# Pairs of token groups in 64x64 quarters instead of single groups, in a retention and MLP kernel

## The chip, the cores and the metric

The kernel runs on one core of one Trainium2 chip. The metric is the device time of one execution in microseconds (us). The four runs of the kernel before lie between 297.73 and 299.04 us. The engines are named as the profile names them: PE is the matrix engine, PEld its weight loads, DVE the vector engine (VectorE in the text), ACT the scalar engine (ScalarE), POOL is GpSimd, SP the engine whose queue (SPq) issues most of the DMA transfers (186 of the 196 issues counted in the trace of the kernel before). "Clock" is the PE clock that the profile gives as granted: 1.0 is full speed.

## The reference

The reference is a decayed, causal attention without a softmax, and an MLP with the activation h cos(h). There are 8 sequences of 576 tokens with 8 heads of 64, so 4608 tokens of 512 features. Cut to what matters:

```python
scores = scale * np.matmul(q, k.transpose(0, 1, 3, 2))
gamma = 1.0 - 2.0 ** (-5.0 - np.arange(H, dtype=np.float32))
Dmat = np.where(rel >= 0, gamma[:, None, None] ** rel[None, :, :], 0.0)
ret = scores * Dmat[None, :, :, :]
attn_out = np.matmul(ret, v)                  # 8 x 8 x 576 x 64
x = attn_out.transpose(0, 2, 1, 3).reshape(B * S, H * D)
h = x @ w_in                                  # 4608 x 2048
g = h * np.cos(h)
out = g @ w_out                               # 4608 x 512
```

## The kernel before

The decay is split into a factor for the query and one for the key, so that only a triangular mask is left for the scores. The tokens are treated in chunks. For a chunk the kernel needs the scores of its own tokens (`sc`), their product with the values (`ov`, "own"), a contribution of all earlier tokens from a state (`ov`, "carried"), and the update of that state (`st`). For all of these the queries and keys are scaled (`qks`) and transposed (`qkT`), in the first groups by PE and later by DMA transfers; this is what "transposes" means below. The result `xT` feeds the first product of the MLP (`h`), ScalarE and VectorE make `gT` of it, and the second product (`o`) follows. PE writes its products into banks of the PSUM memory (named by letters), and here a bank is written again only after its content has been read. The tokens run through the MLP in ten passes of 512, 256, 256 and seven times 512 tokens. From pass 3 on, the second product uses seven half-size products instead of eight; the sums that this needs (`gs`) are made on VectorE and GpSimd.

Before the change a chunk is a group of 128 tokens, one token per partition.

```python
    def load(g, names="qkv", gate=None):          # cut
        for name in names:
            f = ld.tile([P, H, D], F32, tag="f" + name, name=f"f{name}")
            for p0, p1, t in parts:
                b, s0 = divmod(t, S)
                i = nc.sync.dma_start(
                    f[p0:p1], src[b, :, s0 : s0 + p1 - p0, :].rearrange("h s d -> s h d")
                )

    def prep(g, early=False, kv_first=False):     # cut: scales q and k into bf16, copies v
        if not early and not kv_first:
            scaled(nc.gpsimd, 0, tiles.pop(("fq", g)), gq)
        scaled(nc.vector if g == 3 else nc.gpsimd, 1, fk, gk)
        ...

    def scores(g, bank, idle=0, parts=1, put_off=None):   # cut
        warm(ps[:, 0].rearrange("p b i -> p (b i)"), idle)     # dummy matmuls on zeros
        for hg in range(HG):
            for i0 in range(0, P, P // parts):
                for he in range(2):
                    d0, i1 = he * D, i0 + P // parts
                    nc.tensor.matmul(
                        ps[i0:i1, he, hg, :],
                        lhsT=qkT[d0 : d0 + D, HG + hg, i0:i1],
                        rhs=qT[d0 : d0 + D, hg, :],
                        start=True, stop=True)

    def mm1(n, et, c0, w, bank, inside={}):       # first product of the MLP
        m = 1024 // w
        ps = psum.tile([P, m, w], F32, tag=bank, name="h")
        for j in range(m):
            if j in inside:
                inside[j]()
            for dg in range(DG):
                nc.tensor.matmul(ps[:, j, :],
                    lhsT=w_in_sb[:, dg, (et + j) * P : (et + j + 1) * P],
                    rhs=xT[:, dg, c0 : c0 + w],
                    start=(dg == 0), stop=(dg == DG - 1))
        nc.scalar.activation(cosh, ps, ACTF.Sin, bias=half_pi, scale=1.0)
        nc.vector.tensor_mul(gT[:, et : et + m, c0 : c0 + w], ps, cosh)

    # the start: groups 0 to 3 one by one, with dummies that keep PE busy
    warm(psum.tile([P, 512], F32, tag="n", name="idle"), 14)
    ...
    prep(0, early=True)
    transposes(0, "nn", only=(1,))
    scores(0, "a", idle=2)
    for g in range(G4):
        ...
        w_dma += [load_w_in(e, e + 512) for e in ((0,), (512,), (1024, 1536), ())[g]]
        if g == 2:
            w_dma += [load_w_out(e, e + 4) for e in range(0, ET, 4)]
            load(4, gate=w_dma[5])            # not before the weights
            load(5)
        if g + 1 < G4:
            state(g)
            transposes(g + 1, "nn", only=(1,))
            if g + 2 < G4:
                prep(g + 2, early=True)
            scores(g + 1, "ab"[(g + 1) % 2], idle=3)
            attn_out([g], "m", evac=nc.scalar.copy)
    for g in (4, 5):
        prep(g)                               # on GpSimd
    # the passes follow: mm1 of pass 0 and so on
```

## Time and profile before

| | before |
|---|---|
| time, median of 3 runs | 297.98 us (297.73 to 299.04) |
| span of the profiled run | 296.6 us, clock 1.000 |
| PE busy | 285.2 us, 96% |
| VectorE, ScalarE, GpSimd busy | 70%, 46%, 67% |
| first `h` matmul | 17.61 us |

The first lines are from the page of the kernel before. Its first line gives the busy time of each engine, the share of the span, and the number of instructions. Below are slices: each digit is one fortieth of the span, in tenths of busy time (9 is 90% or more), for PE, for the granted PE clock, and for the DMA engines.

```profile
PE 285.2 (96%) x3091; PEld 195.6 (66%) x3113; DVE 208.9 (70%) x245; ACT 135.9 (46%) x167; POOL 199.7 (67%) x163
...
PE   7899999999989999999999999999999999999995
...
PEclk9999999999999999999999999999999999999999
DMA  8999999999999999999999999997850260021013
```

PE is nearly always busy and always at full clock. The DMA engines are busy nearly to the full through the 27th slice, some 200 us, and then the loads are over. The view of waits, for PE alone, gives what PE stood for, in total, how often, and the longest:

```profile
PE idle L185 <- DVE zeros L660: 1.3, 1, 1.3
PE sc L195 <- DMA qkT<-qks: 1.2, 1, 1.2
PE o L515 <- DVE ot L557: 1.0, 4, 0.4
...
```

So PE waits for about 6 us in all, and the longest wait is 1.3 us. A change helps if it shortens the PE stream or the start. The timeline of PE gives start, duration, the line, what is written and read, the PE tile (rows times columns), the shape, the count, and in brackets the idle time before it with its cause. First pass 0:

```profile
17.61 1.05 PE L365 MATMUL h<-xT,w_in_sb 128*128 128x256 bf16 x8
...
19.49 13.26 PE L365 MATMUL h<-xT,w_in_sb 128*128 128x256 bf16 x120
32.59 9.88 PE L382 MATMUL o<-w_out_sb,gT 128*128 128x512 bf16 x44
```

The first product of pass 0 starts at 17.61 us and the second at 32.59 us. The stretch of retention of one late pair of groups, between two products of pass 7, is:

```profile
223.48 0.44 PE L266 MATMUL st<-vb,qks 128*64 128x64 bf16 x16
223.75 0.62 PE L333 MATMUL ov<-ret,vb 128*64 128x128 bf16 x16
224.30 0.42 PE L319 MATMUL ov<-qkT,sb 64*64 64x128 bf16 x16
224.54 0.62 PE L195 MATMUL sc<-qkT 64*64 64x128 bf16 x32
225.09 0.94 PE L515 MATMUL o<-w_out_sb,gT 128*128 128x256 bf16 x7
```

It lasts from 223.48 to 225.09 us, 1.61 us. Four groups of matmuls stand in it, two in 128x64 tiles and two in 64x64 quarters. This is the time that the change wants to shorten.

### The profile page before, as it was taken

Reading aid. Unit: us, or ns where it says so; the run is one execution under the profiler, and the core shown is the slowest. Engines: PE = TensorE matmul, PEld = TensorE weight load, DVE = VectorE, ACT = ScalarE, POOL = GpSimd, SP = SyncE. Lnnn points to the kernel's source line nnn. Section 1 sums busy time; section 2 is a strip of 40 time slices with the busy share of each in tenths; the row PEclk is TensorE's granted clock in tenths of the full one; section 3 lists DMA queues with packets and bytes.
Section 4 is the critical chain, followed back from the end, with each engine's and each line's share of the span. In section 5 each row is a group of like instructions: output and inputs, shape, how many; then the busy total and the mean of one; then the engine's idle time right before and its main releaser. Section 6 shows DMA issues by size and latency. Waiting matters only on the chain. (4 is left out here: it accounts for less than half of the span.)

```text
span 296.6 us, 7311 instructions
## 1 busy us (share of the span) xinstructions
PE 285.2 (96%) x3091; PEld 195.6 (66%) x3113; DVE 208.9 (70%) x245; ACT 135.9 (46%) x167; POOL 199.7 (67%) x163
## 2 busy tenths in 40 slices
PE   7899999999989999999999999999999999999995
PEld 3478646848568887468745784488448844884594
DVE  6677647564669995688758975897589758935873
ACT  3656432605236532663256355636464446425620
POOL 2750056544445789999999998599859935970583
PEclk9999999999999999999999999999999999999999
DMA  8999999999999999999999999997850260021013
GB/s 208 213 210 207 210 197 201 210 210 232 201 160 232 199 243 231 216 283 160 198 217 254 212 213 221 200 223 194 180 140 2 73 144 0 2 81 62 0 38 106
DMA packets 154304, 50.28 MB, mean 170 GB/s; under 512 B 140832, under 2 KB 153248, under 8 KB 154272
## 3 DMA queue, kind: packets, MB, share of 16 engines
q1 hardware_dynamic: 149504, 45.10, 77.9%
q0 software_dynamic: 4224, 4.19, 8.5%
q8 instruction: 24, 0.39, 0.5%
q10 hardware_dynamic: 544, 0.52, 0.5%
q14 instruction: 8, 0.07, 0.1%
HBM read 36.70 MB, written 9.44 MB: 156 GB/s over the span
## 5 line engine op out<-in xcount | busy, mean ns | idle before, releaser
L443 POOL TENSOR_TENSOR gs<-gT 128x1024 bf16<-128x1024 bf16 x51 | 107.1, 2131 | 36.1 <-DVE gs L443 35.5
L365 PE MATMUL h<-xT,w_in_sb 128*128 128x512 bf16 (+2 forms) x820 | 126.8, 313 | 1.3 <-DVE xT L350 0.7
L374 DVE TENSOR_TENSOR gT<-h,cosh 128x1024 bf16<-128x1024 f32 x72 | 87.9, 1223 | 45.5 <-ACT cosh L373 43.0
L373 ACT ACTIVATE cosh<-h,half_pi 128x1024 f32<-128x1024 f32 x72 | 80.2, 1114 | 66.9 <-PE h L365 66.9
L365 PEld LDWEIGHTS <-w_in_sb 128*128 128x128 bf16 x832 | 75.9, 98 | 49.5 <-issue 1.0
L140 POOL TENSOR_TENSOR qks<-fq,gq 128x512 bf16<-128x512 f32 x32 | 34.2, 1068 | 40.0 <-DMA fq<-in_q_dram 33.7
L515 PEld LDWEIGHTS <-gs 128*128 128x128 bf16 x576 | 53.9, 98 | 9.5 <-issue 1.7
L140 POOL TENSOR_TENSOR qks<-fk,gk 128x512 bf16<-128x512 f32 x35 | 37.7, 1076 | 9.4 <-DMA fk<-in_k_dram 8.8
L207 DVE TENSOR_TENSOR ret<-sc,tri 128x1024 bf16<-128x1024 f32 x32 | 38.1, 1215 | 2.7 <-PE sc L195 2.7
L515 PE MATMUL o<-ws,gs 128*128 128x256 bf16 (+1 forms) x352 | 38.8, 268 | 0.1
L382 PE MATMUL o<-w_out_sb,gT 128*128 128x512 bf16 x120 | 28.9, 380 | 0.5 <-issue 0.2
L515 PE MATMUL o<-w_out_sb,gs 128*128 128x256 bf16 x224 | 26.3, 272 | 1.0 <-DVE ot L557 1.0
L515 PE MATMUL o<-w_out_sb,gT 128*128 128x256 bf16 x224 | 26.3, 273 | 0.0
L535 DVE TENSOR_TENSOR ot<-o,ot 128x512 f32<-128x512 f32 (+2 forms) x25 | 14.9, 603 | 13.9 <-PE o L515 13.8
L515 PEld LDWEIGHTS <-gT 128*128 128x128 bf16 x224 | 21.5, 98 | 4.2
L350 ACT CAST xT<-ov 128x1024 bf16<-128x1024 f32 (+1 forms) x18 | 16.5, 917 | 16.0 <-PE ov L319 13.9
L443 DVE TENSOR_TENSOR gs<-gT 128x1024 bf16<-128x1024 bf16 (+1 forms) x18 | 21.1, 1187 | 0.3
L382 PEld LDWEIGHTS <-gT 128*128 128x128 bf16 x128 | 11.8, 98 | 12.5
L156 POOL CAST vb<-fv 128x512 bf16<-128x512 f32 x22 | 13.8, 628 | 5.1 <-DMA fv<-in_v_dram 3.3
L562 ACT COPY ot<-o 128x512 f32<-128x512 f32 x7 | 4.1, 586 | 20.2 <-PE o L515 20.2
L392 ACT COPY ot<-o 128x512 f32<-128x512 f32 x8 | 4.7, 588 | 18.5 <-PE o L382 18.4
L195 PEld LDWEIGHTS <-qkT 64*64 64x64 bf16 (+1 forms) x512 | 9.0, 105 | 6.1 <-ACT qkT L177 2.3
(70 smaller groups left out, 176.1 us busy)
## 6 DMA issues: line engine op xcount, KB each, us to landing
out_dram<-ot SPq DMA_DIRECT2D x35, 256.0 KB, 4.0
fk<-in_k_dram SPq DMA_DIRECT2D x32, 256.0 KB, 5.1
fv<-in_v_dram SPq DMA_DIRECT2D x32, 256.0 KB, 5.1
fq<-in_q_dram SPq DMA_DIRECT2D x30, 256.0 KB, 4.5
w_in_sb<-in_moe_w_in_dram POOLq DMA_DIRECT2D x4, 512.0 KB, 8.9
w_out_sb<-in_moe_w_out_dram POOLq DMA_DIRECT2D x4, 512.0 KB, 16.3
fq<-in_q_dram SPq DMA_DIRECT2D x8, 128.0 KB, 4.0
fk<-in_k_dram SPq DMA_DIRECT2D x8, 128.0 KB, 4.1
```

The lines of the kernel that those rows point to most:

```text
L140: eng.tensor_tensor(out=qks[:, m].rearrange("p (b a) d -> p a b d", a=2), in0=f.rearrange("p (a b) d -> p a b d", a=2), in1=by[:, c, :].re ...
L156: copy_v(vb, fv)
L195: nc.tensor.matmul(ps[i0:i1, he, hg, :], lhsT=qkT[d0 : d0 + D, HG + hg, i0:i1], rhs=qT[d0 : d0 + D, hg, :], start=True, stop=True,)
L207: nc.vector.tensor_tensor(out=ret.rearrange("p a b i -> p (a b) i"), in0=ps.rearrange("p a b i -> p (a b) i"), in1=mask.unsqueeze(1).to_br ...
L350: evac(tiles["x", n][:, :, t0 : t0 + len(gs) * P], ps.rearrange("p c x i -> p c (x i)"))
L365: nc.tensor.matmul(ps[:, j, :], lhsT=w_in_sb[:, dg, (et + j) * P : (et + j + 1) * P], rhs=xT[:, dg, c0 : c0 + w], start=(dg == 0), stop=(d ...
L373: nc.scalar.activation(cosh, ps, ACTF.Sin, bias=half_pi, scale=1.0)
L374: nc.vector.tensor_mul(gT[:, et : et + m, c0 : c0 + w], ps, cosh)
L382: nc.tensor.matmul(ps, lhsT=gT[:, et, tsi * P : (tsi + 1) * P], rhs=w_out_sb[:, et, :], start=(et == 0), stop=(et == ET - 1),)
L443: i = (nc.vector if on_dve else nc.gpsimd).tensor_tensor(out=tiles["gs", n, x][:, e0:e1], in0=i0, in1=i1, op=op_)
L515: nc.tensor.matmul(dst[i], lhsT=lhs[:, e, j * P : (j + 1) * P], rhs=rhs[:, e, c0:c1], start=(x in (3, 4, 1, 7) and e == 0 and (i == 0 or l ...
L535: pend.append(lambda: nc.vector.tensor_tensor(out=out_, in0=in0, in1=in1, op=op_))
```

## The change

Groups are taken in pairs, 18 of them. In the first six (`FINE = 6`), partition p holds two neighbouring tokens, so one DMA packet has 512 bytes instead of 256 (the page counts 140832 packets under 512 bytes before); their chunks stay at 128 tokens. In the other twelve the chunks shrink to 64 tokens. So less is computed above the diagonal, more states are made, and every product of the retention is a 64x64 quarter of the array, so four of them run beside each other. Some of the half sums move from GpSimd to VectorE, where one takes 0.69 us at the median instead of 2.13 us on average. The start treats pairs 0 and 1 as wholes and has fewer dummies. The diff is long; its core, with cuts marked:

```diff
+    NP = NG // 2
+    QP = P // 4
+    NC = S // HP
+    FINE = 6
-    LD = 5
+    LD = 3
...
-            f = ld.tile([P, H, D], F32, tag="f" + name, name=f"f{name}")
-            for p0, p1, t in parts:
-                b, s0 = divmod(t, S)
+            f = ld.tile([P, H, 2, D], F32, tag="f" + name, name=f"f{name}")
+            for rows, ys, b, s0, cnt in parts:
+                n = ys.stop - ys.start
                 i = nc.sync.dma_start(
-                    f[p0:p1], src[b, :, s0 : s0 + p1 - p0, :].rearrange("h s d -> s h d")
+                    f[rows, :, ys, :].rearrange("p h r d -> p h (r d)"),
+                    src[b, :, s0 : s0 + cnt, :].rearrange("h (p r) d -> p h (r d)", r=n),
                 )
...
+    def prep(G, y, engines=None, copy_v=None):
+        eng = engines or nc.gpsimd
+        if G >= 2:
+            scaled(eng, 0, tiles["fq", G], gq)
+        scaled(eng, 1, tiles["fk", G], gk)
...
+                for hg in range(HG):
+                    for x in range(2):
+                        for he in range(2):
+                            nc.tensor.matmul(
+                                ps[half(x), he, blocks_of(G, u, hg), :],
+                                lhsT=qkT[half(he), u, HG + hg, half(x)],
+                                rhs=queries(G, he, hg, x, yq),
+                                start=True,
+                                stop=True,
+                            )
...
+            for x in range(2):
+                evac(xT[:, x], outs[x])
...
         on_dve = x == 5 or (n, x) == (S7, 2) or (n, x, e0) in (
-            (S7, 1, 4), (last, 1, 0), (last, 2, 4)
-        )
+            (S7, 1, 4), (S7 + 1, 2, 4), (last, 1, 0), (last, 2, 4)
+        ) or (x == 6 and e0 == 0 and S7 < n < last)
...
+    prep(0, 0, copy_v=False)
+    w_dma.append(load_w_in(0, 512))
+    key_transposes(0, "m")
+    masks0 = scores(0, idle=1)
...
+    w_dma += [load_w_in(e, e + 512) for e in (1024, 1536)]
+    w_dma += [load_w_out(e, e + 4) for e in range(0, ET, 4)]
+    load(2, gate=w_dma[5])
+    load(3)
+    load(4)
+    key_transposes(1, "m")
+    run, done = retention(0)
+    run("cross", True)
+    run("own")
+    run("same")
+    done()
+    masks1 = scores(1)
...
+    prep(2, 0)
+    prep(2, 1, nc.vector)
+    prepared = transposed = 6
+    run1, done1 = retention(1, ("n", "st"))
...
             inside = {
-                (0, 0): {2: lambda: (attn_out([3], "n"), state(3))},
-                (1, 0): {4: lambda: scores(5, "a")},
-                (1, 1): {3: lambda: attn_out([5], "a", evac=nc.scalar.copy)},
+                (0, 0): {2: lambda: run1("own"), 3: lambda: run1("same", True)},
+                (0, 1): {0: lambda: (run1("cross"), done1())},
+                (3, 0): {3: lambda: carry(5, ("n", "st"))},
             }.get((n, i), {})
```

## The prediction

It was made from the code, the diff and the profile before, without building the change.

> **What bounds it now.** TensorE. The page's busy table gives PE 285.2 of 296.6 us (96%), at full granted clock in all slices. The waits view, for PE alone, lists only about 6 us of idle: 1.3 before the first matmul, 1.2 on a DMA transpose, 1.0 (four times) on a VectorE add before a product, 0.7 on an xT copy, 0.5 on a state add. The chain of waits is matmuls too. So a saving counts only if it shortens the PE stream, one of these holes, or the start (first h matmul at 17.6 us in the timeline). VectorE is at 70%, GpSimd 67%; the DMA is about 99% busy until some 195 us (slices), yet costs PE only that 1.2 us.
>
> **PE stream of a pair.** In the timeline one late pair (states, values, carried, scores, between two products) lasts 1.5 to 1.7 us, e.g. 223.48 to 225.09. Starts of single matmuls in the trace at 171.3-172.9 us: two 128x64 matmuls of 64 columns every 31 ns, of 128 columns every 56 ns; four 64x64 quarters of 128 columns every 56 ns, of 64 columns every 28 ns. Going from 128x64 to 64x64, and from 64x64 to 128x128, cost about 92 ns more each. [...]
>
> Late pairs (12 of 18), before: states 0.27, values 0.50, carried 0.24, scores 0.50, plus switches: 1.6 us. After: 32 quarters of 64 columns in each of four parts, eight fours at 28-31 ns = 0.24 us each, 0.96, plus two switches: estimate 1.15 us. More instructions, fewer streamed columns. Saving 0.45 x 12 = 5.4 us, all critical.
>
> First six pairs: quarters keep 128 columns: about 1.5 us, as now. Pairs 0-2 now run by single groups in half-array forms (about 2.2 us per pair without transposes): 0.5 us each saved. The 256-token pass in 128-column blocks (128 at 61 ns) becomes 64 at about 110 ns: 0.7 us.
>
> **Others.** The 32 recorded masks of 1.22 us fall to 24; two more state adds per late pair; about six half sums of 2.1 us leave GpSimd for VectorE [...]. Should remove half of the mid-kernel holes (3.7 us): 1.5 us. New holes (a semaphore step between row groups, begin/end splits that switch mode again, sums just in time): minus 1.5 us.
>
> **Start.** Packets go from 256 to 512 bytes: medians in the trace are 18 and 27 ns, so the first keys and values should all land near 13 us, not 16. But a pair now needs both halves' keys scaled, transposed, copied and masked before its first use; first h matmul near 16.5 us, then stalls for pair 1. I credit 0.5 us.
>
> Sum: 5.4 + 1.5 + 0.7 + 1.5 - 1.5 + 0.5 = about 8 us.
>
> **Prediction: 290.0 us, 8 in 10 between 286.0 and 294.5.** Faster by over 2% (below 292.0): 0.72; within 2%: 0.25; slower: 0.03.
>
> **What would show it.** Late retention stretches near 1.15 us; four 64-column quarters every 28-31 ns; first h matmul at 16-17 us; DMA busy share below 90% before 60 us; PE waits 5 us or less in total; 24 masks; N=512 and N=256 matmuls unchanged.
>
> **What would make it wrong.** Quarters of 64 columns with a weight load each may be limited by loads (0.4 us per part would leave no saving). The order of parts may make PE wait for masks or state copies, most in the start and passes 0 to 2. Sums gated behind VectorE could come late for the products. The start could be better than I credit by 2 us.

The sum stays at 8.1 us. Its 0.5 us for each of pairs 0 to 2, its 1.5 us for the mid-kernel holes, its minus 1.5 us for new ones and its 0.5 us for the start were guesses and not read from a trace.

## The result and the profile after

A ratio in this document is the mean time of one kernel's runs over that of the other's runs of the same rounds, so it is not quite the ratio of the medians that stand beside it. Executions over 1.5% slower than the fastest of the same kernel are left out of the means.

| | before | after |
|---|---|---|
| time, median | 298.42 us (297.73 to 299.04, 4 runs) | 322.10 us (321.32 to 323.28, 4 runs) |
| ratio, 95% interval | | 1.0798 (1.0753 to 1.0842) |
| span and clock of the profiled run | 296.6 us, 1.000 | 320.1 us, 0.957 |
| PE busy | 285.2 us | 287.3 us |

The change made the kernel 8% slower, where 290 us were predicted. The same lines of the page after:

```profile
PE 287.3 (90%) x3827; PEld 195.9 (61%) x3848; DVE 199.3 (62%) x252; ACT 148.4 (46%) x194; POOL 190.1 (59%) x173
...
PE   8597059997999989899898998999999999999995
...
PEclk9857659999999999999999999999999999999999
DMA  8999999199999990599959999998793133022003
```

A slice is now 8.0 us. PE has a hole in the fifth and sixth slices, 32 to 48 us. The clock is not full in the second to sixth slices. The waits of PE after:

```profile
PE h L491 <- DVE gT L500: 13.8, 4, 11.5
PE h L491 <- ACT xT L440: 4.1, 3, 1.9
...
```

One wait of 11.5 us is new, on VectorE's `gT`. The timeline of PE in pass 0 of the kernel after shows where:

```profile
18.62 1.87 PE L491 MATMUL h<-xT,w_in_sb 128*128 128x256 bf16 x8
...
26.64 5.21 PE L491 MATMUL h<-xT,w_in_sb 128*128 128x256 bf16 x31 [1.91 <-ACT xT L440]
43.38 11.24 PE L491 MATMUL h<-xT,w_in_sb 128*128 128x256 bf16 x80 [11.53 <-DVE gT L500]
54.45 0.38 PE L508 MATMUL o<-w_out_sb,gT 128*128 128x512 bf16 x1
```

The second product starts at 54.45 us instead of 32.59 us. The wait names VectorE, so the next question is what VectorE waited for. Its timeline in this stretch:

```profile
39.07 0.69 DVE L158 TENSOR_TENSOR qks<-fq,gq 128x512 bf16<-128x512 f32 x1 [18.25 <-DMA fq<-in_q_dram]
41.50 0.69 DVE L158 TENSOR_TENSOR qks<-fk,gk 128x512 bf16<-128x512 f32 x1 [1.74 <-DMA fk<-in_k_dram]
```

VectorE stood for 18.25 us, and not for any `h` that it was to make into `gT`. It stood for the queries of pair 2. Its queue holds `prep(2, 1, nc.vector)` before the first `gT`, because that line is above the loop of passes in the program. The keys of the same pair were issued, in the timeline of the SP queue, at

```profile
32.17 1.53 SPq L137 DMA_DIRECT2D fk<-in_k_dram  x2
```

which is behind the weights, as the gate on `load(2)` wants. The chain of waits, read in order of time (start, length, what), runs through all of it:

```profile
17.69 13.58 DMA w_out_sb<-in_moe_w_out_dram
...
32.17 0.53 SPq L137
32.75 8.66 DMA fk<-in_k_dram
41.50 0.69 DVE qks L158
42.19 1.14 DVE gT L500
43.38 9.50 PE h L491 x64
```

(The short pieces named "issue", and the issue of the load of the queries at 31.29 us, are left out.) Weights, then the issue of the load of pair 2's keys, then their transfer, then the scaling on VectorE, then the first `gT`, then PE. PE could fill three banks with `h` (48 matmuls), and then stood until one was read.

The late stretch of retention of the kernel after, for pass 7 as before:

```profile
248.35 0.32 PE L414 MATMUL ov<-qkT,sb 64*64 64x64 bf16 x16
248.50 0.43 PE L245 MATMUL sc<-qkT 64*64 64x64 bf16 x32
248.80 0.44 PE L414 MATMUL ov<-ret,vb 64*64 64x64 bf16 x32
249.07 0.30 PE L414 MATMUL ov<-qkT,sb 64*64 64x64 bf16 x16
249.20 0.44 PE L316 MATMUL st<-vb,qks 64*64 64x64 bf16 x24
249.56 1.92 PE L643 MATMUL o<-w_out_sb,gT 128*128 128x256 bf16 x16
```

It lasts from 248.35 to 249.56 us, 1.21 us against 1.61 us; the other stretch of this pass takes 1.17 us (254.91 to 256.08) against 1.56 us (230.76 to 232.32). Fours of quarters start every 31 to 33 ns, by the starts of single matmuls in the trace. So the intended gain exists. The starts of the first `h` matmul of each pass, read from the timeline of PE, say where the sum was lost. The two right columns belong to experiments below, E1 and E14.

| start, us | before | after | after minus before | E1 minus before | E14 minus before |
|---|---|---|---|---|---|
| pass 0, `h` | 17.61 | 18.62 | +1.0 | +1.1 | 0.0 |
| pass 0, `o` | 32.59 | 54.45 | +21.9 | +6.3 | 0.0 |
| pass 1, `h` | 48.97 | 73.33 | +24.4 | +8.8 | 0.0 |
| pass 2, `h` | 67.28 | 90.64 | +23.4 | +7.8 | 0.0 |
| pass 3, `h` | 85.06 | 106.96 | +21.9 | +7.5 | -0.7 |
| pass 4, `h` | 116.92 | 140.54 | +23.6 | +9.2 | -0.5 |
| pass 5, `h` | 147.90 | 173.07 | +25.2 | +10.8 | -0.7 |
| pass 6, `h` | 178.14 | 203.94 | +25.8 | +11.6 | +2.7 |
| pass 7, `h` | 207.82 | 232.70 | +24.9 | +10.7 | +1.7 |
| pass 8, `h` | 237.57 | 261.33 | +23.8 | +9.6 | +0.6 |
| end | 296.6 | 320.1 | +23.5 | +9.3 | +0.5 |

Nearly all of the 23.5 us arises before the second product of pass 0. From pass 6 to pass 8 the kernel after wins back 2.0 us for four pairs (59.43 us become 57.39 us), or 0.51 us a pair, near the predicted 0.45 us. By the windows view, 0.40 us of this is a shorter PE stream (58.77 us of busy time in passes 6 and 7 become 57.18 us) and 0.11 us less waiting. But in passes 3 to 5, where six late pairs were to gain as well, it loses 3.9 us more. The windows view for these three passes (start and end, length, then busy time of PE, PEld, DVE, ACT, POOL with counts, the clock, the DMA share, GB/s; this share adds up the times of all packets that start in the window, so it can pass 1), first before, then after:

```profile
85.06:116.92 31.86, 31.58 (x449) 27.02 (x448) 25.86 (x34) 15.42 (x19) 23.69 (x19) 1.00 1.23 216
116.92:147.90 30.98, 30.36 (x353) 19.97 (x353) 23.39 (x25) 13.61 (x16) 30.07 (x24) 1.00 1.11 215
147.90:178.14 30.24, 29.75 (x337) 19.94 (x337) 23.16 (x24) 15.97 (x21) 28.84 (x24) 1.00 1.12 225
```

```profile
106.96:140.54 33.58, 31.45 (x569) 26.71 (x568) 23.91 (x33) 17.29 (x24) 14.14 (x10) 1.00 0.65 135
140.54:173.07 32.53, 29.89 (x480) 19.98 (x480) 26.23 (x33) 15.92 (x21) 28.70 (x25) 1.00 0.99 181
173.07:203.94 30.87, 29.20 (x415) 19.52 (x417) 20.55 (x26) 17.04 (x23) 25.10 (x20) 1.00 1.08 208
```

PE was busy for 91.69 us before (31.58 + 30.36 + 29.75) and for 90.54 us after: the stream is shorter. But the windows last 93.08 us and 96.98 us. PE's idle time went from 1.4 to 6.4 us (length minus busy time). The saving in this part turned into waits.

### The profile page after: what moved, and what is told of

Same layout as the page of the kernel before. It is cut to its first block, busy times and chain, and to the rows that moved or that the text cites. A ratio compares the mean times of both kernels' runs of the same rounds, so it can differ in the third digit from the quotient of the medians.

```text
span 320.1 us, 8840 instructions
## 1 busy us (share of the span) xinstructions
PE 287.3 (90%) x3827; PEld 195.9 (61%) x3848; DVE 199.3 (62%) x252; ACT 148.4 (46%) x194; POOL 190.1 (59%) x173
## 2 busy tenths in 40 slices
DMA packets 137718, 50.38 MB, mean 157 GB/s; under 512 B 107856, under 2 KB 136656, under 8 KB 137680
## 4 chain that ended last, share of the span: by engine, by line
PE 71%; DMA 11%; DVE 6%; POOL 4%; ACT 3%; issue 2%; SPq 1%; DVEq 0%; POOLq 0%; ACTq 0%
PE h L491 33%; PE o L643 23%; PE o L508 9%; DMA fk<-in_k_dram 5%; DMA w_out_sb<-in_moe_w_out_dram 4%; PE ov L414 3%; DVE gT L500 2%; POOL gs L569 2%; ACT cosh L499 2%; PE sc L245 2%; PE st L316 1%; DMA qkT<-qks 1%; DVE gs L569 1%; DVE s L339 1%; SPq L137 1%
## 5 line engine op out<-in xcount | busy, mean ns | idle before, releaser
L491 PE MATMUL h<-xT,w_in_sb 128*128 128x256 bf16 (+1 forms) x756 | 133.1, 335 | 20.1 <-DVE gT L500 13.8
L569 POOL TENSOR_TENSOR gs<-gT 128x1024 bf16<-128x1024 bf16 x45 | 94.4, 2127 | 69.9 <-DVE gs L569 66.7
L491 PEld LDWEIGHTS <-w_in_sb 128*128 128x128 bf16 x768 | 77.2, 101 | 72.5 <-issue 21.1
L158 POOL TENSOR_TENSOR qks<-fq,gq 128x512 bf16<-128x512 f32 x31 | 33.2, 1071 | 45.0 <-DMA fq<-in_q_dram 17.4
L668 DVE TENSOR_TENSOR ot<-o,ot 128x512 f32<-128x512 f32 (+2 forms) x32 | 19.7, 620 | 12.4 <-PE o L643 11.8
L440 ACT CAST xT<-ov 128x512 bf16<-128x512 f32 x36 | 20.8, 637 | 13.1 <-PE ov L414 12.8
L347 ACT CAST sb<-s 128x768 bf16<-128x768 f32 (+2 forms) x16 | 10.5, 659 | 21.6 <-DVE s L339 19.3
L569 DVE TENSOR_TENSOR gs<-gT 128x1024 bf16<-128x1024 bf16 (+1 forms) x24 | 19.5, 841 | 0.4
L668 DVE TENSOR_TENSOR ot<-ot,o 128x512 f32<-128x512 f32 x14 | 9.6, 687 | 10.5 <-ACT ot L698 8.3
L261 DVE TENSOR_TENSOR ret<-sc,tri 128x1024 bf16<-128x1024 f32 x10 | 11.9, 1219 | 5.6 <-PE sc L245 5.6
L257 DVE TENSOR_TENSOR ret<-sc,tri 128x1024 bf16<-128x1024 f32 x12 | 14.6, 1214 | 0.0
```

The lines of the kernel that those rows point to most:

```text
L158: eng.tensor_tensor(out=qks[:, y, m].rearrange("p (b a) d -> p a b d", a=2), in0=f[:, :, y, :].rearrange("p (a b) d -> p a b d", a=2), in1 ...
L257: nc.vector.tensor_tensor(out=ret, in0=ps, in1=by, op=ALU.mult)
L261: nc.vector.tensor_tensor(out=ret.rearrange(shape, r=2), in0=ps.rearrange(shape, r=2), in1=by.unsqueeze(1).to_broadcast([P, H, P]), op=ALU ...
L440: evac(xT[:, x], outs[x])
L491: nc.tensor.matmul(ps[:, j, :], lhsT=w_in_sb[:, dg, (et + j) * P : (et + j + 1) * P], rhs=xT[:, dg, c0 : c0 + w], start=(dg == 0), stop=(d ...
L569: i = (nc.vector if on_dve else nc.gpsimd).tensor_tensor(out=tiles["gs", n, x][:, e0:e1], in0=i0, in1=i1, op=op_)
```

## The experiments

The first theories were these. T1: the scaling of pair 2 on VectorE, in front of the `gT` of pass 0, made the hole, because VectorE works in the order of its queue (it stood 18.25 us at that scaling). T2: the start leaves PE idle so much, with fewer dummies, that the clock falls to half (from 14.1 to 24.3 us in the kernel after) and the first pass runs cold. Rivals for the hole and the rest were the moved half sums, the size of the packets, and the gated loads themselves. Where a text uses T5, it is that a VectorE sum takes 2.75 us instead of 0.69 us because GpSimd works beside it without a gap; T6 is the order of transposes and loads in the SP queue; another number stands for one of the rivals just named. All kernels of this section gave correct results. Those of one batch share the runs of the kernel before; its medians were 299.18, 299.09, 299.24, 299.23 and 299.18 us in the five batches.

### E1: the scaling of pair 2's second half later on VectorE

```diff
     prep(2, 0)
-    prep(2, 1, nc.vector)
...
             ] + [
+                (20, lambda: prep(2, 1, nc.vector)),
                 (42, lambda: transposes(2, 0, "a")),
```

The same instructions run on the same engine, but now in the second product of pass 0.

> Changed kernel with one move: VectorE scales the second half of pair 2 after the last h*cos(h) of the first pass instead of before the first. Theory T1 (the strictly ordered VectorE queue stands behind that scaling, which waits until 41.5 us for keys that are loaded after the weights): the 11.5 us hole in PE goes, and with it the half clock that followed (about 2.2 us on 80 matmuls), so 308 us, between 305 and 311; PE waits on gT below 3 us in total. Rival R1 (the DMA cannot bring pair 2 and the weights in time, so the next user of the data would wait instead): 318 us or more, PE waiting on a DMA or on GpSimd for about as long. Rival R2 (64x64 quarters and their mode changes cost the time): 320 us or more.

Measured: 308.73 us median (307.66 to 310.77, 4 runs), ratio 1.0340 (1.0289 to 1.0390). PE's waits in this kernel:

```profile
PE h L491 <- ACT xT L440: 3.9, 3, 1.7
PE h L491 <- DVE gT L500: 2.3, 3, 1.2
...
```

The hole is gone, and with it some 13 us. The column for E1 in the table above shows it: +21.9 us became +6.3 us at the second product of pass 0. The half clock at the start stayed (14.7 to 25.0 us in the clock records), so T2 isn't part of the hole, but of what is left.

### E2: the scaling on GpSimd

```diff
     prep(2, 0)
-    prep(2, 1, nc.vector)
+    prep(2, 1)
```

> Changed kernel, both halves of pair 2 scaled by GpSimd, which has nothing urgent there. T1: as e1, 308 us, between 305 and 312; the transposes of pair 2 may come 1 to 2 us later than in e1. R1 and R2: 318 us or more.

Measured: 307.96 us (one run, state unknown). It's the same as E1 within what one run can tell. So it isn't the place in time, but the queue that the waiting instruction stands in. GpSimd may wait there; VectorE may not.

### E3: pair 2 without the gate

```diff
-    load(2, gate=w_dma[5])
+    load(2)
```

The scaling stays on VectorE and in front of pass 0; only its data come earlier.

> Changed kernel, the scaling left where it was, but the loads of pair 2 no longer wait for the weights. T1: VectorE is released when the keys land, around 15 to 20 us, so the hole that ends with a gT is under 2 us; but 4.5 MB go ahead of or beside the weights, so PE should wait for weights instead: 305 to 318 us. R1: no gain or worse, 320 us or more, with the wait merely renamed to a weight DMA. R2: 320 us.

Measured: 308.67 us (one run). This removes the same amount from the other side. PE's waits on `gT` are 2.3 us in total, as in E1, and the later weights cost PE only 0.7 us. So the hole needs both parts: late data, and an in-order queue with urgent work behind.

### E4: the same mistake in the kernel before

```diff
-        scaled(nc.vector if g == 3 else nc.gpsimd, 1, fk, gk)
+        scaled(nc.vector if g in (3, 5) else nc.gpsimd, 1, fk, gk)
```

Group 5 is loaded behind the weights, and its keys are scaled above the loop of passes.

> The kernel before, with one edit: the keys of group 5 are scaled by VectorE instead of GpSimd, at the same place ahead of the first pass. T1: a hole of 8 to 11 us appears in PE in the first pass, ended by a gT, 307 to 312 us in all, and the granted clock drops after it. R1 and R2: unchanged within 1%, 296 to 301 us.

Measured: 325.97 us (one run), 26.8 us more than the median of before. The hole was larger than expected, its cause as T1 says. In the timelines of this kernel, of VectorE and of PE:

```profile
43.76 0.69 DVE L140 TENSOR_TENSOR qks<-fk,gk 128x512 bf16<-128x512 f32 x1 [24.70 <-DMA fk<-in_k_dram]
```

```profile
45.11 5.11 PE L365 MATMUL h<-xT,w_in_sb 128*128 128x256 bf16 x28 [24.38 <-DVE xT L350]
```

In the kernel before VectorE also holds the `xT` copy of group 3 behind the scaling, so PE stood from 20.7 us on, for 24.4 us. The clock records show half clock from 25.1 to 49.0 us, so about 3.9 us of work after the hole ran at half speed. One line that moves 0.69 us of work to another engine costs 27 us: this settles T1.

### E8: the kernel before without its dummies

```diff
-    scores(0, "a", idle=2)
+    scores(0, "a", idle=0)
...
-            scores(g + 1, "ab"[(g + 1) % 2], idle=3)
+            scores(g + 1, "ab"[(g + 1) % 2], idle=0)
```

> The kernel before without its eleven dummy matmuls ahead of the scores of groups 0 to 3. T2: the clock falls to half between 14 and 18 us [...] and the kernel takes 301 to 304 us. R3: the clock stays full, 297 to 299.5 us, as it has few quarters there.

Measured: 301.85 us (one run), 2.8 us more than the batch's median of before; clock at half from 12.5 to 22.8 us. The eleven dummies do no work for the result and are worth about 2.8 us in the kernel before. So T2 is real in size, and in the kernel before it is paid by dummies.

### E5: E1 with dummies at the start

```diff
-    masks0 = scores(0, idle=1)
+    masks0 = scores(0, idle=3)
+    spare = psum.tile([P, 512], F32, tag="st", name="idle")
...
+    warm(spare, 2)
     key_transposes(1, "m")
+    warm(spare, 4)
```

> e1_late plus ten dummy matmuls of 512 columns in the start, at places where PE stands idle between 10 and 15.5 us. Theory T2 (PE does too little there, since the change runs pair 0 as a whole and keeps only two of nine dummies, so the granted clock falls to half at about 14.7 us and stays there for 10 us; that costs 3 to 5 us of matmul time): clock full throughout, matmuls of 256 columns at 19 us every 110 ns instead of 230 ns, 304.5 us, between 303 and 306.5. Rival R3 (the half clock comes with the 64x64 quarters themselves, or the start waits for data and not for the clock): clock falls all the same, or 307.5 us and more.

Measured: 307.70 us median (305.76 to 310.44, 4 runs, one of them slow), ratio 1.0263 (1.0218 to 1.0308). The clock is full until 25.3 us, and the first eight `h` matmuls take 1.03 us instead of 1.87 us. But of the expected gain only about 2 us are there, and the interval overlaps that of E1. So the half of R3 that ties the clock to the quarters is refuted, but by its time E5 falls on R3's side: with full clock, PE still waits at the start for `xT`, for a state and for `xT` again (0.73, 1.01 and 1.96 us). The profiled run was the slow one; it has half clock at 25.3 to 28.8 us, just behind the wait of 1.96 us at 24.6 us, and again at 90.2 to 93.6 us. The first of these isn't due to the slow state: E11 below has the same start, took 305.94 us, and shows the same waits and half clock from 25.4 to 28.8 us. The second isn't there. (The recorded text counts nine dummies in the kernel before, as its trace does; the program has eleven.)

### E6: E1 with the half sums where they were

```diff
-            (S7, 1, 4), (S7 + 1, 2, 4), (last, 1, 0), (last, 2, 4)
-        ) or (x == 6 and e0 == 0 and S7 < n < last)
+            (S7, 1, 4), (last, 1, 0), (last, 2, 4)
+        )
```

The order of the sums in `sums_after` and `late_sums` goes back too.

> e1_late with the half sums of the seven-product passes put back to the engines and the order of the kernel before. If the moved sums cause the new waits in passes 4 and 5 (1.2 us on a gT, 0.5 us on a carry, 1.4 us on a masked score): these go and it takes 306.5 us, between 305.5 and 307.5. If the moved sums were needed by the new order: the products wait for GpSimd, 310 us or more. If they don't matter: within 0.5 us of e1_late.

Measured: 307.57 us (307.34 to 308.21, 4 runs), ratio 1.0284 (1.0260 to 1.0308). The intervals of E6 and E1 overlap, so no difference is shown, though the ratio of E6 lies just below the interval of E1 and the median 1.2 us below that of E1. The two profiled runs differ in the clock at the start too (6.8 us at half clock in E6, 10.2 us in E1). So the moved sums are at most a small part of the loss, and they show no gain.

### E7: E1 with three instead of six pairs of two tokens per partition

```diff
-    FINE = 6
+    FINE = 3
```

Pairs 3 to 5 then have chunks of 64 and packets of 256 bytes.

> e1_late with only pairs 0 to 2 loaded with two tokens per partition; pairs 3 to 5 in chunks of 64 with 256-byte packets. If the larger packets of pairs 3 to 5 matter (they shorten these loads): waits on DMA transposes grow in passes 1 to 3 and it takes 2 us or more longer, 310.5 to 313. If only the PE stream matters: 64-column quarters save about 0.4 us in each of three pairs, so 307.5 us, between 306.5 and 308.5.

Measured: 313.19 us (311.38 to 316.50, 4 runs, one slow), ratio 1.0505 (1.0433 to 1.0577), against 1.0340 for E1 in another batch. PE now waits 5.1 us in all for the transposes that the DMA makes (3.7 us the longest), against 2.1 us in all in E1. The edit changes the chunks as well as the packets, but PE was busy for less time than in E1 (282.7 against 284.2 us), so the loss is one of waiting; that it comes from the packets is argued and not shown: this run has no measure of the packets alone. The DMA records of the two main traces have one: in the first 20 us a packet of 256 bytes took 24.3 ns on average in the kernel before, and one of 512 bytes 33.4 ns in the kernel after, so some 1.45 times as many bytes in the same time.

### E11: E5 with the half sums of pass 4 made later on VectorE

```diff
         elif n == S7 + 1 and i in (3, 7):
-            for x in (5, 2):
-                g_sum(n, x, i - 3, i + 1)
+            if i == 7:
+                g_sum(n, 5, 0, 4)
+                g_sum(n, 5, 4, E2)
+            g_sum(n, 2, i - 3, i + 1)
```

The reason was one line of VectorE's timeline. The same sum took 0.69 us before and 2.75 us in E1:

```profile
126.44 0.69 DVE L443 TENSOR_TENSOR gs<-gT 128x1024 bf16<-128x1024 bf16 x1
```

```profile
135.61 2.75 DVE L569 TENSOR_TENSOR gs<-gT 128x1024 bf16<-128x1024 bf16 x1
```

In E1, GpSimd runs two scalings (of two inputs each) and a copy in turn, without a gap, from 124.99 to 137.8 us, and the sum ends 0.54 us after that. In the kernel before GpSimd had a gap of 0.28 us where the sum began.

> e5_warm with one change: in pass 4 the first half sum that VectorE makes in the middle of the pass (2.75 us there, 0.69 us in the kernel before) is made at the end of the pass. Theory T5 (that sum takes four times as long because GpSimd runs two-input operations without a gap beside it; this delays the next gT and PE waits 1.2 us): the gT wait of 1.2 us in pass 4 goes, and no VectorE sum there takes over 1.5 us unless GpSimd runs two-input operations beside it. Rival (VectorE is simply full): the wait stays.

Measured: 305.94 us (one run). The wait of 1.2 us on `gT` in pass 4 is gone. The two lines above agree with T5; what the two engines hold from each other is not shown. The 2.75 us are no fixed factor, though: in the kernel after the same sum takes 2.73 us and ends 0.55 us after GpSimd's unbroken stretch, so it looks as if it was held until GpSimd paused. This sum is on VectorE in the kernel before as well; it isn't one of those that the change moved. Only one run was made, so the gain in time isn't established.

### E9: E5 with the halves of xT apart

```diff
+    def halves(xT):
+        return xT.rearrange("p c i -> p (c i)").rearrange("p (h c i) -> p h c i", h=2, c=DG)
...
-            xT = tiles["x", n][:, :, t0 : t0 + 2 * P]
+            xT = halves(tiles["x", n])[:, t0 // 256] if n in (0, 3) else (
+                tiles["x", n][:, :, t0 : t0 + 2 * P]
+            )
...
-                    rhs=xT[:, dg, c0 : c0 + w],
+                    rhs=(
+                        halves(xT)[:, c0 // 256, dg, :] if n in (0, 3) else xT[:, dg, c0 : c0 + w]
+                    ),
```

In pass 0 the second block of `h` reads only the first half of the columns, but it waited for the copy of the second half. The addresses of the two halves interleave, so the dependency may be one of ranges and not of data. The edit puts the halves one after the other.

> e5_warm with one change of layout: in passes 0 and 3 the two halves of xT lie one after the other instead of interleaved by feature block. Theory T4 (the second h matmul of the second block waits 1.96 us, and one in pass 3 0.83 us, for a copy into the other half of xT, because the written and the read addresses interleave and the dependency is drawn over the whole range): both waits move to the first matmul that really reads the second half and shrink together by about 2 us; as PE then has no such hole, the clock should not fall at 25 us either (1.7 us). About 303.5 us, between 302 and 306. Rival (the copy is really needed, or the start is late for other reasons): same waits, 305.5 us or more.

Measured: 308.72 us (307.28 to 309.16, 4 runs), ratio 1.0304 (1.0269 to 1.0340): no gain in the whole. The line of the next `h` matmuls in PE's timeline, first E5, then E9, shows that the wait itself did go:

```profile
24.63 13.94 PE L491 MATMUL h<-xT,w_in_sb 128*128 128x256 bf16 x111 [1.96 <-ACT xT L440]
```

```profile
24.61 10.64 PE L496 MATMUL h<-xT,w_in_sb 128*128 128x256 bf16 x96 [0.32 <-ACT xT L445]
```

The main part of the second product of pass 0 starts at 35.96 us instead of 39.29 us. So 3.3 us were won; a part of it is the half clock from 25.3 to 28.8 us in that run of E5, which E9 doesn't have. (E5's profile is of its slow run; E11, with the same start, has the same wait of 1.96 us and starts this part at 39.25 us.) And then:

```profile
89.05 1.07 PE L245 MATMUL sc<-qkT 64*64 64x128 bf16 x32 [3.48 <-DMA qkT<-qks]
```

PE waits 3.48 us for the transposes of pair 5, and has half clock from 87.9 us, still within the wait, to 94.7 us. In E1 this wait was 0.91 us and ended at 89.66 us, in E11 1.17 us and ended at 89.43 us, in E5's slow run 2.15 us and ended at 90.45 us. Whatever PE gains before, it goes on at 88 to 90 us. That is a second bound, one of supply: the data of pair 5 aren't loaded, scaled and transposed earlier. And the half clock that came with this wait took back more of what was won.

### E10: E9 with six more repairs of order

It reorders the blocks of pass 0, gives pass 1 other banks, takes pair 2 and pair 5 earlier, makes the first half sum of pass 4 later (as E11 does), and makes a mask of pass 4 before the states. Some of the edit:

```diff
-    when = {0: 3, 1: 4, 3: 5, 4: 6, 6: 7}
+    when = {0: 3, 1: 4, 2: 5, 4: 6, 6: 7}
...
-                (0, 0): {2: lambda: run1("own"), 3: lambda: run1("same", True)},
-                (0, 1): {0: lambda: (run1("cross"), done1())},
+                (0, 1): {0: lambda: run1("own"), 2: lambda: run1("same", True)},
+                (0, 2): {0: lambda: (run1("cross"), done1())},
```

> e9_layout with the remaining waits taken out one by one: three blocks of pair 0 run before pair 1 is needed, another PSUM bank for the third h block of pass 1, pair 2 begun two matmuls and finished four matmuls earlier, pair 5 prepared one tile earlier, the first half sum of pass 4 made at the end of the pass, and in the last third of pass 4 the mask before the state sums. By the waits in the profile of e5_warm: 1.0 carry, 0.8 gT, about 0.9 xT, 2.1 transpose, 1.2 gT, 1.3 ret, so about 7 us less than e9_layout: 297 us, between 293 and 300, so about as fast as the kernel before or a little faster. If the waits only turn into others: 301 us or more.

Measured: 305.27 us (303.03 to 308.25, 6 runs, one slow), ratio 1.0176 (1.0142 to 1.0211). It has the lowest median of the versions with the whole change. The transposes cost PE 6.0 us in the profiled run (which was the slow one), the two longest waits being 2.58 us at 89.6 us and 2.23 us at 181.8 us.

### E12 and E13: the order in the SP queue, and the values of pair 2

E12 is E10 with the transposes put into the SP queue in front of the loads, at both places that issue them; the first is:

```diff
-        while loaded < min(NP, G + LD, prepared // 2 + LD):
-            load(loaded)
-            loaded += 1
         while prepared < 2 * G + 2:
...
             transposed += 1
+        while loaded < min(NP, G + 1 + LD, prepared // 2 + LD):
+            load(loaded)
+            loaded += 1
```

E13 is E12 with the values of pair 2's second half copied on VectorE, and the sums of the weights moved into passes 1 and 2.

```diff
-                (20, lambda: prep(2, 1, nc.vector)),
+                (33, lambda: prep(2, 1, nc.vector, nc.vector.tensor_copy)),
```

> e10_best, but the transposes of pairs already scaled are put into the SyncE queue ahead of the next loads, as the kernel before has it, instead of after them. Theory T6 (the transposes stand in the queue behind loads that wait for buffers and for the full DMA): the waits of scores for transposes at 67, 89 and 182 us (6 us in e10_best) fall below 1.5 us together, 300.5 us, between 298.5 and 302.5. Rival (the DMA is simply too full): waits move to the loads and it stays at 303.5 us or more.

> e12_order, with the values of the second half of pair 2 copied by VectorE instead of GpSimd and the sums of w_out made in passes 1 and 2 instead of 0. The wait of 1.5 us for the copy of the straddling values at 49 us goes: 1 to 1.5 us less than e12_order, 299 us. If VectorE then holds up the masks of pair 2, no gain.

Measured: E12 305.62 us (305.22 to 306.58, 4 runs), ratio 1.0211 (1.0166 to 1.0255). The same wait in E12:

```profile
88.01 1.07 PE L245 MATMUL sc<-qkT 64*64 64x128 bf16 x32 [4.96 <-DMA qkT<-qks]
```

It is longer and not shorter, and the whole time for transposes is 6.0 us as in E10. So T6, the order in this queue, is rejected as the cause. E13 has 306.22 us (304.71 to 307.04, 4 runs), ratio 1.0214 (1.0172 to 1.0256). The wait of 1.5 us for a copy of the values, which E10 had at 49 us, is gone, but it was down to 0.23 us in E12 already, so that isn't E13's doing. The waits for transposes grew to 7.3 us. No gain is shown.

### E14: the late pairs alone

This is the kernel before up to pass 2, with its own loads, start and dummies, and from pass 3 on the twelve late pairs in chunks of 64 and in quarters, with the change's order in passes 3 to 9, E11's order of the sums and E10's order of the mask in pass 4. The edit has some 400 lines of diff; its joint is:

```diff
+    def to_fine():
+        attn_out([10, 11], "b", nc.scalar.copy)
+        states([11])()()
+        tiles["sb64", (FINE - 1, 1, 1)] = tiles["sb", 12]
...
-            late += [lambda: unit(g + 2, "b", False)]
+            late += [to_fine]
```

> The kernel before up to pass 2, with single groups, its loads, its start and its dummies, and only the twelve later pairs in the form of the change (chunks of 64 in 64x64 quarters, with the change's order inside passes 3 to 9, its moved half sums, and the two mends of pass 4 from e10_best). If the step of the prediction about late pairs holds (0.45 us each, on PE): 293.5 us, between 291 and 296, against 299 for the kernel before; each pass from 6 on about 1 us shorter. If the late form brings waits of its own that eat the saving: 297 us or more.

Measured: 298.04 us (297.22 to 300.96, 6 runs), ratio 0.9959 (0.9918 to 1.0001). The interval just touches one, so it isn't shown to be faster. It is 10.7 us faster than E1, and the fastest kernel with any part of the change. So most of what remained in E1 doesn't come from the quarters of the late pairs, but from pairs 0 to 5 and what follows from them. Why don't its twelve pairs bring 5 us? The table's last column tells: from pass 6 to pass 8 it wins 2.1 us, as the kernel after does. In pass 5 it loses 3.5 us, at one wait:

```profile
166.44 0.32 PE L378 MATMUL sc<-qkT 64*64 64x64 bf16 x16 [3.18 <-DMA qkT<-qks]
```

Half clock follows from 167.9 to 171.4 us. The kernel before has no wait at this place.

### E15 and E16: pass 5's data earlier, and a cap on the loads

E15 is E14 with the groups of pass 4 scaled and transposed one store earlier. E16 adds a cap on the loads at the end of pass 3. The first line is shortened.

```diff
-            while prepared < min(NG, ... + ((0, 1, 2, 4) if n else (-1, 0, 1, 4))[r]):
+            while prepared < min(NG, ... + ((1, 2, 3, 4) if n == 1 else (0, 1, 2, 4) if n else (-1, 0, 1, 4))[r]):
...
-            ahead = starts[S7] // P + 14 if n == 0 and r < 3 else prepared + LD
+            ahead = starts[S7] // P + 14 + (2 if r == 3 else 0) if n == 0 else prepared + LD
```

> e14_late_only, but in pass 4 each group is scaled and transposed one store earlier. If the 3.2 us wait for the transposes at 166 us is only their place in the queues, it goes, with the half clock behind it (about 1.7 us): 294 us, between 292 and 296. If the transposes can't come earlier, since GpSimd and the DMA are full there: 297 to 299 us, with the wait still above 2 us.

> e15_early, and at the end of pass 3 only four groups of loads instead of up to nine are put into the SyncE queue, so that the first transposes of pass 4 stand ahead of the others. Same alternatives as e15_early; if loads ahead of the transposes in the queue are what holds them, this one is the faster of the two: 293 us, between 291 and 295. If the loads then come too late for pass 6: waits on fq or fk, 297 us or more.

Measured: E15 303.72 us (302.23 to 304.85, 6 runs), ratio 1.0154 (1.0121 to 1.0187). In its timeline of PE:

```profile
165.76 0.32 PE L378 MATMUL sc<-qkT 64*64 64x64 bf16 x16 [1.02 <-DMA qkT<-qks]
...
178.27 0.43 PE L378 MATMUL sc<-qkT 64*64 64x64 bf16 x16 [5.65 <-DMA qkT<-qks]
```

The wait at 166 us fell from 3.18 to 1.02 us, and a new one of 5.65 us came 12 us later, with half clock from 175.6 to 182.4 us. E16 has 305.88 us (304.76 to 306.71, 6 runs), ratio 1.0228 (1.0199 to 1.0256), with waits of 3.89 and 4.40 us. Shifting the order moves the waits and makes the sum worse. What bounds the supply of transposed pairs before 200 us is left open: the transfers, the scaling on GpSimd and the SP queue are all in that path, and no run here takes one of them out alone. The DMA slices show the transfers busy until then, which makes them the likely one; that is argued and not shown. No version clearly beats the kernel before.

## Why the prediction was wrong

**The step that failed** is in the last paragraph of the prediction: "The order of parts may make PE wait for masks or state copies, most in the start and passes 0 to 2." It stood there as a risk; the term for it in the sum is "New holes", "minus 1.5 us", beside a credit of 0.5 us for the start. One new hole alone measured 11.5 us, and some 13 us with the half clock behind it (E1). What made PE wait was neither a mask nor a state copy, but an input scaling in the VectorE queue whose data come after the weights. The code that was read says all of it: the line `prep(2, 1, nc.vector)` stands above the loop of passes, and `load(2, gate=w_dma[5])` above that. The prediction counted VectorE's busy time, 70%, and never walked its queue in program order. The trace shows what that order cost: VectorE stood 18.25 us and 1.74 us before two scalings of 0.69 us each, while finished `h` lay in three banks.

Point by point:

- **PE bounds the kernel, so only the PE stream, its holes or the start count.** Right for the kernel before. After the change there was a second critical path, through the loads, the scaling and VectorE.
- **Late pairs, 0.45 us each.** Right in size: 0.51 us a pair in passes 6 and 7 (59.43 to 57.39 us over four pairs), 0.40 us of it in the PE stream. Wrong in reach. In passes 3 to 5 the PE stream shrank by 1.2 us, and PE's idle time grew by 5.0 us. E14 shows the same without the early part: 2.1 us won in passes 6 and 7, 3.5 us lost in pass 5 to a wait for transposes.
- **First six pairs, 1.5 us, and the 256-column blocks, 0.7 us.** Seen in part, and hidden by the rest. Passes 1 and 2 together took 36.09 us before, 33.63 us after and 34.80 us in E1; PE's busy time in them fell from 33.77 to 32.09 us. But E1 without the hole is still 6.3 us late at the second product of pass 0 and 7.5 us at pass 3, while E14, with the old form of these pairs, isn't.
- **Start, +0.5 us of gain, first `h` at 16.5 us.** Wrong: 18.62 us, and at half clock from 14.1 to 24.3 us. The diff shows the fewer dummies; the prediction gave them no price. E8 puts 2.8 us on the dummies in the kernel before.
- **Mid-kernel holes, 1.5 us.** Wrong in sign. The waits of PE outside the hole grew; the moved half sums showed no gain (E6), and another half sum, on VectorE before and after, took 2.73 us instead of 0.69 us.
- **What would show it.** The late stretches came near the 1.15 us: 1.17 and 1.21 us in pass 7. Masks did fall from 36 to 24 recorded ones (the prediction said 32, having missed the four mixed ones). Matmuls of 256 and 512 columns are unchanged in the groups: 273 and 379 ns after, 273 and 380 ns before. Fours of quarters start every 31 to 33 ns, at and above the upper end of the 28 to 31 ns. The DMA share does fall below 90% before 60 us (0.00 from 56 to 60 us by the windows view), but that is no sign of a gain: the hole held up everything by then. E1, without the hole, has no such slice from its second to its 14th, some 107 us. PE waits of 5 us or less show in none of the versions with the whole change.
- **"Quarters of 64 columns with a weight load each may be limited by loads."** This named risk didn't come true: in the stretch shown, a part of eight fours took 0.27 to 0.30 us, not 0.4 us.

The sum of 23.5 us, as far as runs settle it: about 13.4 us (322.1 minus 308.7 us, medians of two batches) for the hole with the clock that falls behind it; about 2 us for the cold start (E5 against E1, intervals overlapping); the rest, about 8 us, is not taken apart by runs. It is spread over pass 0 (an address dependency worth up to 3.3 us locally, with the clock behind it, E9), pair 2, and the waits for transposes. E9, E10, E12 and E13 show that repairs there are paid back, in whole or in part, at the next wait for data.

The long wait was paid twice here. The clock records of the kernel after have half clock from 14.1 to 24.3 us, from 27.7 to 31.1 us and from 34.6 to 48.2 us (10.2, 3.4 and 13.7 us); E9 had 6.8 us of it at 87.9 us, and E4 23.9 us around its hole. After its hole, PE of the kernel after went on at 43.38 us and the clock rose at 48.21 us. From this, an estimate: 4.8 us at half speed lose about 2.4 us.

## What to carry to other kernels

Before you move an operation to a less busy engine, write down that engine's queue in program order and give each entry the time when its data arrive; a short instruction with late data holds everything behind it (here 0.69 us of scaling held PE for 11.5 us). Put it on an engine whose queue may wait, or behind the urgent work. And where PE hides a data supply that is nearly at its limit, a faster PE only meets the next wait sooner (3.48 us for the transposes of pair 5 in E9, 0.91 us in E1), and half clock can come behind a short wait as well (1.91 us in the kernel after, 3.18 us in E14; the last section has more); test a saving alone, as E14 does, before you join it with a new start.

## What the traces show besides

- Half clock came behind short waits too: it follows a wait of 1.91 us in the kernel after (27.7 to 31.1 us) and one of 1.96 us in E11 (with other waits of 0.73 and 1.01 us in the 7 us before), while E9, with 0.73, 1.01 and 0.32 us at the start, kept its full clock there, the kernel before kept it behind a wait of 1.16 us that ended at 83.19 us, and E10 behind one of 2.58 us that ended at 89.55 us (1.00 in the windows view from 85 to 95 us). So the length of the last wait alone doesn't decide it; what does is not shown.
- For four 64x64 quarters the traces show starts 3 to 4 ns apart and a four every 31 to 33 ns, so 8 ns each on average.
- In the trace of the kernel before a change between 128x64 and 64x64, or back to the full array, cost about 92 ns more than the usual step (150 ns at 224.30 us and 148 ns at 225.09 us, where 56 ns are usual).
- A bf16 sum of 128x1024 on VectorE took 0.69 us where GpSimd had a gap of 0.28 us, and 2.75 us (E1) and 2.73 us (kernel after) beside GpSimd operations without one; in the kernel after it outlasted three of them, and the two sums ended 0.54 and 0.55 us after the last.
- PE waited up to 5.65 us (E15) for transposes made by the DMA where the windows view gives a DMA share of 1.22 (150 to 200 us), and the order in the queue didn't explain it (E12, 4.96 us in one wait).
